# Attention over selected blocks, then a token and channel mixer, on one core: splits and word copies that a planner may put on GpSimd or on VectorE

## The chip, the cores and the metric

The kernel runs on one core of a Trainium2 chip. A core has TensorE (PE, matrix products into PSUM), VectorE (DVE), ScalarE (ACT), GpSimd (POOL) and SyncE (SP, which here only issues DMAs). Each engine takes its instructions from its own queue, in the order in which the program wrote them, and waits for the others through semaphores. The metric is the device time of one execution in microseconds, as the median of several runs.

## The reference

```
q, k, v: [4, 8, 768, 64]                    batch, heads, sequence, head size
kbar  = mean of k over blocks of 64          12 blocks
gate  = q . kbar                             later blocks are left out
sel   = the 3 best blocks of each query, and its own block
attn  = softmax(q k^T / 8 where the key's block is in sel and key <= query)
x     = attn v, heads side by side           [4, 768, 512]
u     = x + (relu(x^T w_tok1) w_tok2)^T
out   = u + relu(u w_ch1) w_ch2
```

## The kernel before

**Pairs.** Two heads of one batch form a pair; there are 16 pairs, number i = 0 to 15, four to a batch. With two heads of 64 channels side by side, a pair's q and k fill 128 partitions once they are transposed. For each pair the kernel loads q, k and v, brings q and k into the layout with channels on partitions, sums k over its blocks, multiplies q by these sums (the gates, tile gps), finds the third largest of the 12 gates of each query (top, tile m), turns "smaller than that" into a bias (bn), transposes the bias, and puts it as 12 extra rows beside q in the tile Q. KA holds k with 12 indicator rows. So the matrix product of KA and Q gives the scores with the mask already in them (sps, L683). ACT takes the exponential (e, L697), PE multiplies by V (aps, L713; a column of ones gives the sum), DVE normalises (rc L721, x L732).

**Mixer.** After the four pairs of a batch come the token mixer (tok1 L756 or L787, umix L768 or L801, uadd L776 or L810) and the channel mixer: a first product (ch1, L837) with relu (L739, L741), and a second one (L888), which is done as seven products of half size per row block, with sums of their operands before (hsum, L869 to L875) and of their results after (keep L745 or L747, vsum L903, vu L910 on POOL, oput L922 and L924, psum L928 and osum L933 on POOL). The mixer of one batch runs between the pairs of the next.

**How k is brought in and split.** Three ways stand side by side:

- Pairs below SPLIT (0 and 1): transposes of f32 data in two halves into PSUM banks (L417), evacuation to f32 tiles kt and qt by ACT or DVE (L443, L445), block sums by DVE into kst, two DVE reductions that write them into the tile ks2 with zeros elsewhere (kcopy, L566), and gates as five f32 matmuls per pair against ks2 (gate_full, L575).
- Pairs from SPLIT to QTURN/KTURN: transposes of six blocks at once into one of the two big PSUM tiles (L409), k evacuated to f32 (L443 or L445), q evacuated as an f16 main part qh (ACT, L458) and an f16 rest qr (DVE, L465). The block sums are split likewise into an f16 main part and an f16 rest in the tile kp (split_k, L549). The gates are ten f16 matmuls (gate_parts, L591), qh and qr against kp.
- Later pairs (q from pair 10, k from 14, the bias from 9): the f16 parts are made before the transposition (L514, L520, L445/L479), which a DMA then does (L399 for u, L525, L640).

kp has a column group for each head of the pair, and a partition of the one head holds zeros in the column group of the other. split_k therefore writes only the 64 x 12 values of each head: four POOL instructions, main part and rest for two heads. The zeros are written once at the start (L1406).

**Word copies.** qh, kh and mt arrive as f16 and must go to the rows of Q and KA. place_q (L546), place_k (L491) and place_m (L646) copy them as f32 words, on POOL.

**Who decides the order.** The kernel first lists all operations, each with an engine, a duration as the planner believes it (occ until the engine is free, rec until the result can be used), its dependencies, a priority and the buffers that it takes. plan() then simulates the engines and picks, step by step, the operation that can start first; among those that can start within NEAR ns of it, the one with the lowest priority value. An operation with an `alt` can go to either of two engines, whichever the plan has done first. `both` marks a DVE operation that the planner does not start before POOL's last instruction has nearly ended. The result is one fixed order per engine; nothing is decided on the chip. PRE (per pair), LAG (per batch) and SHIFT (per kind of operation) move priorities. W0 and WAIT name the copies behind which POOL issues each load of the weights. Dummy matmuls (L963) keep PE busy at the start until 17 us.

Of the kernel before, what the change touches and what calls it, by code (L numbers as in the profile page):

```python
# [45 lines left out]
SHIFT = {'bias': 0.7, 'sc': -0.8999999999999999, 'ex': -2.2, 'uadd': 1.0, 'lt': 4.2, 'ch1': -0.8, 'qn2': 0.0, 'av': 2.8, 'tok1': -11.0, 'gate': -0.5, 'qr': 1.2999999999999998, 'mask': -2.8, 'ksum': -0.3, 'cast': -1.0, 'dg': 2.7, 'half': 1.3, 'top': 0.2, 'put': 0.0, 'kt': -4.0, 'gm': -2.7, 'norm': 4.3999999999999995, 'kcopy': 0.0, 'tr': 0.5, 'v': -0.8, 'relu2': 1.0, 'umix': -0.5, 'relu1': 1.0, 'qh': -6.8, 'qn': -1.5}  # L46
# [17 lines left out]
NEAR = 20.0  # L64
SEED = 0
JITTER = 0.0
SPLIT = 2
# [36 lines left out]
def plan(ops, rings, near=NEAR):  # L104
# [43 lines left out]
    while left:  # L148
# [7 lines left out]
        for e, cand in ready.items():  # L156
# [9 lines left out]
            for op in cand:  # L166
# [51 lines left out]
        if op.both:  # L218
            both_to = t + op.rec
# [31 lines left out]
def kernel(  # L251
# [69 lines left out]
    two = sp.tile([128, 2], F16, tag="two", name="two")  # L321
    spare = sp.tile([128, 8], F16, tag="spare", name="spare")
# [165 lines left out]
    def place_k(i, x):  # L488
        def f():
            lo = 64 * x  # L490
            nc.gpsimd.tensor_copy(out=KA[i % R][x][lo:lo + 64, :].bitcast(FP), in_=T["kh", i][lo:lo + 64, :].bitcast(FP))  # L491
        return f
# [50 lines left out]
    def place_q(i, x):  # L543
        def f():
            lo = 64 * x
            nc.gpsimd.tensor_copy(out=QA[i % R][x][lo:lo + 64, :].bitcast(FP), in_=T["qh", i][lo:lo + 64, :].bitcast(FP))  # L546
        return f

    def split_k(i):  # L549
        def f():  # L550
            kst = T["kst", i]
            t = kp[i % 2]
            for c in range(2):
                for x in range(2):
                    rows = slice(64 * x, 64 * x + 64)
                    hi, lo = t[rows, 1 - x, 0, :], t[rows, 1 - x, 1, :]
                    if c == 0:
                        nc.gpsimd.tensor_copy(out=hi, in_=kst[rows, :])
                    else:
                        nc.gpsimd.tensor_tensor(out=lo, in0=kst[rows, :], in1=hi, op=ALU.subtract)  # L560
# [82 lines left out]
    def place_m(i, x):  # L643
        def f():
# [807 lines left out]
```

## Time and profile before

| | us |
|---|---|
| median of 3 runs | 248.72 (248.71 to 248.92) |
| profiled execution, device time | 249.24 |
| its span, first to last instruction | 247.5 |

The profile is one execution. Its page gives for each engine the busy time and its share of the span; other views of the trace give the same by stages of the span, by line and operation ("L546 POOL COPY Q<-qh 64x384 f32<-64x384 f32 x28" is the copy of line 546, from qh to Q, 64 partitions by 384 words, 28 times, followed by total time, mean in ns, and the idle time of the engine before it with what ended it), and in order of time. A matrix instruction's recorded duration includes its way through the pipeline, so on PE the difference of two starts says what an instruction costs, and the recorded duration says more.

Some shares of the chain of work that ended last:

| by engine | share of the span |
|---|---|
| PE | 67% |
| DMA | 9% |
| POOL | 7% |
| DVE | 5% |
| SP's queue | 4% |
| ACT | 4% |

### The profile page before, as it was taken

How to read it: one execution, taken by the hardware profiler on the slowest of the kernel's cores; microseconds unless marked ns; L12 is line 12 of the kernel's file. 1: busy time of each engine (PE TensorE's matmuls, PEld its weight loads, DVE VectorE, ACT ScalarE, POOL GpSimd, SP SyncE). 2: the span in 40 equal slices, each digit the busy share in tenths (PEclk: the TensorE clock that was granted, in tenths of full speed). 3: DMA queues.
4: the chain of work that ended last, by engine and by line, in shares of the span. 5: the costliest groups of instructions: out<-in, count | busy, mean ns of one | idle time of the engine just before them, and what ended most of it. 6: DMA issues, size and time to landing. Idle time of an engine off the chain costs nothing.

```text
span 247.5 us, 6749 instructions
## 1 busy us (share of the span) xinstructions
PE 237.5 (96%) x2590; PEld 180.2 (73%) x2590; DVE 184.8 (75%) x568; ACT 157.8 (64%) x239; POOL 133.8 (54%) x234
## 2 busy tenths in 40 slices
PE   8998899999999999999999989999999999999994
PEld 6777789877777886687767868658676758756863
DVE  6668569979688997997978999896754659442742
ACT  2778797887996898564566668668759321345210
POOL 8658557369018836577793789994010053800380
PEclk9999999999999999999999999999999999999999
DMA  8999999999993499989999992628200009410033
GB/s 160 211 201 227 185 216 218 216 190 215 230 187 76 103 221 202 192 126 237 231 202 131 213 228 60 157 56 193 47 4 0 3 1 190 153 42 0 3 120 136
DMA packets 106640, 35.78 MB, mean 145 GB/s; under 512 B 100272, under 2 KB 103112, under 8 KB 106608
## 3 DMA queue, kind: packets, MB, share of 16 engines
q1 hardware_dynamic: 101616, 30.84, 62.4%
q0 software_dynamic: 3392, 4.11, 10.1%
q10 hardware_dynamic: 1600, 0.39, 0.8%
q8 instruction: 20, 0.33, 0.6%
q14 instruction: 12, 0.10, 0.1%
HBM read 26.92 MB, written 6.29 MB: 134 GB/s over the span
## 4 chain that ended last, share of the span: by engine, by line
PE 67%; DMA 9%; POOL 7%; DVE 5%; SPq 4%; ACT 4%; issue 2%; POOLq 0%; DVEq 0%; ACTq 0%
PE c L837 24%; PE c L888 13%; PE sps L683 9%; PE aps L713 5%; SPq L360 4%; DMA w<-in_moe_w_tok_dram 3%; DMA ql<-in_q_dram 3%; PE tok L756 3%; POOL vu L910 3%; ACT e L697 3%; DMA v<-in_v_dram 3%; PE tkl L409 2%; PE c L944 2%; PE ups L768 2%; PE tql L409 1%
## 5 line engine op out<-in xcount | busy, mean ns | idle before, releaser
L697 ACT ACTIVATE e<-sps 128x1024 f16<-128x1024 f32 (+2 forms) x96 | 84.7, 918 | 16.7 <-PE sps L683 13.3
L837 PE MATMUL c<-uT,wc 128*128 128x256 f16 (+1 forms) x384 | 68.8, 326 | 0.1
L683 PE MATMUL sps<-Q,KA 76*128 76x128 f16 (+7 forms) x384 | 51.8, 259 | 0.9 <-ACT kt L443 0.3
L910 POOL TENSOR_TENSOR vu<-v,u 128x256 f32<-128x256 f32 x33 | 25.6, 801 | 48.1 <-DVE v L903 46.4
L837 PEld LDWEIGHTS <-wc 128*128 128x128 f16 x384 | 36.4, 98 | 20.4 <-issue 0.5
L683 PEld LDWEIGHTS <-KA 76*128 76x128 f16 (+1 forms) x384 | 30.9, 97 | 14.6 <-issue 1.6
L540 POOL CAST KA<-kt 64x768 f16<-64x768 f32 x26 | 21.8, 837 | 26.5 <-ACT kt L443 22.2
L713 PEld LDWEIGHTS <-e 128*128 128x128 f16 x672 | 24.9, 97 | 2.9 <-issue 0.4
L713 PE MATMUL aps<-V,e 128*128 128x65 f16 x672 | 26.5, 193 | 0.3 <-POOL V L386 0.3
L739 ACT ACTIVATE h2a<-c 128x512 f16<-128x512 f32 (+1 forms) x31 | 16.1, 534 | 13.2 <-PE c L837 13.1
L739 ACT ACTIVATE h2b<-c 128x512 f16<-128x512 f32 (+1 forms) x30 | 15.5, 532 | 11.0 <-PE c L837 10.9
L888 PEld LDWEIGHTS <-s 128*128 128x128 f16 x198 | 18.6, 98 | 2.7 <-DVE s L875 0.3
L386 POOL CAST V<-v 128x768 f16<-128x768 f32 x16 | 14.7, 926 | 7.7 <-DMA v<-in_v_dram 7.0
L732 DVE TENSOR_TENSOR x<-aps,rc 128x384 f16<-128x384 f32 x32 | 17.7, 552 | 0.6
L888 PE MATMUL c<-t,s 128*128 128x256 f16 x132 | 18.0, 272 | 0.0
L703 DVE TENSOR_TENSOR e<-e,m 128x768 f16<-128x768 f16 x24 | 13.8, 575 | 4.8 <-ACT e L697 4.6
L546 POOL COPY Q<-qh 64x384 f32<-64x384 f32 x28 | 16.2, 580 | 2.0 <-ACT qh L458 0.7
L741 DVE TENSOR_SCALAR h2b<-c 128x256 f16<-128x256 f32 (+1 forms) x18 | 8.4, 466 | 9.5 <-PE c L837 9.3
L888 PEld LDWEIGHTS <-h2b 128*128 128x128 f16 x132 | 12.7, 98 | 2.5 <-issue 0.2
L622 DVE MAX8 m<-gps 128x8 f32<-128x12 f32 x160 | 14.0, 161 | 0.4
L613 DVE TENSOR_REDUCE kst<-kt 128x12 f32<-128x768 f32 x13 | 12.3, 944 | 2.6 <-ACT kt L443 2.5
L888 PEld LDWEIGHTS <-h2a 128*128 128x128 f16 x132 | 12.4, 98 | 1.4
(126 smaller groups left out, 428.6 us busy)
## 6 DMA issues: line engine op xcount, KB each, us to landing
v<-in_v_dram SPq DMA_DIRECT2D x16, 384.0 KB, 6.2
out_dram<-ob SPq DMA_DIRECT2D x23, 256.0 KB, 2.2
kl<-in_k_dram SPq DMA_DIRECT2D x30, 192.0 KB, 4.7
ql<-in_q_dram SPq DMA_DIRECT2D x30, 192.0 KB, 4.9
wc<-in_moe_w_ch_dram POOLq DMA_DIRECT2D x8, 384.0 KB, 7.3
w<-in_moe_w_tok_dram POOLq DMA_DIRECT2D x2, 384.0 KB, 6.5
kl<-in_k_dram SPq DMA_DIRECT2D x4, 96.0 KB, 3.2
ql<-in_q_dram ACTq DMA_DIRECT2D x4, 96.0 KB, 3.7
```

Source lines behind the costliest of these rows:

```text
L386: nc.gpsimd.tensor_copy(out=V16[i % (R + 1)][:, :, :, 0:D], in_=T["v32", i])
L540: nc.gpsimd.tensor_copy(out=dst[i % R][x][lo:lo + 64, a:z], in_=T[name, i][lo:lo + 64, a:z])
L546: nc.gpsimd.tensor_copy(out=QA[i % R][x][lo:lo + 64, :].bitcast(FP), in_=T["qh", i][lo:lo + 64, :].bitcast(FP))
L622: nc.vector.max(out=t[:, j, x, :], in_=T["gmx", i, m][:, j, x, :])
L683: nc.tensor.matmul(out=p[:, off + a:off + a + n], lhsT=KA[i % R][x][0:rows, 128 * kk:128 * kk + 128], rhs=QA[i % R][x][0:rows, q0 + a:q0 + ...
L697: nc.scalar.activation(out=e[:, 0:width], in_=T["sps", i, x, g][:, 0:width], func=AF.Exp, scale=scale)
L713: nc.tensor.matmul(out=p[:, jq, :], lhsT=T["e", i, x, g][:, o:o + 128], rhs=V16[i % (R + 1)][:, x, kk, :], start=(kk == 0), stop=(kk == jq))
L732: nc.vector.tensor_tensor(out=T["x16", b][:, :, 64 * hh:64 * hh + 64], in0=T["aps", i, x][:, :, 0:64], in1=T["rc", i, x].broadcast_to([128 ...
L739: e.activation(out=out, in_=src, func=AF.Relu)
L837: nc.tensor.matmul(out=p, lhsT=wc1_16[:, cc, 128 * fc:128 * fc + 128], rhs=T["uT", b][:, a // 128:e // 128, cc, :], start=(cc == 0), stop= ...
L888: nc.tensor.matmul(out=T["c2" + key, b, j], lhsT=x[:, fc, :], rhs=y[:, fc, :], start=first and fc == 0, stop=fc == HF - 1, skip_group_chec ...
L910: nc.gpsimd.tensor_tensor(out=t, in0=T["v", b, j], in1=T["u", b][:, j + 3 * row, 256 * col:256 * col + 256], op=ALU.add)
```

## The change

split_k takes three instructions on all 128 partitions: a product of the block sums with a 0/1 column per head (the new tile half), which puts zeros where the other head's columns are, then the f16 copy, then the rest as a difference. The zeros of kp need no memset any more. split_k, place_q, place_k and place_m become operations of a new kind, flex: planned on POOL, or on DVE where the plan has them done earlier there. For these the rule about DVE and POOL holds where they are planned on DVE. SPLIT goes from 2 to 3, so pair 2 takes the first of the three ways above. NEAR, PRE, LAG and SHIFT have new values.

```diff
-PRE = [3.5, -2.0, -3.0, 0.5, 3.5, 4.0, 5.0, 6.5, -2.5, 0.5, 9.5, 12.5, 3.5, 5.5, -3.0, 2.0]
-LAG = [5.5, 0.0, 3.5, 10.0]
+PRE = [4.0, -1.5, -2.5, 1.0, 3.5, 4.0, 5.0, 6.5, -2.5, 0.5, 9.5, 12.0, 5.5, 7.5, -2.5, 4.0]
+LAG = [5.5, 0.0, 0.5, 7.5]
...
-NEAR = 20.0
+NEAR = 30.0
...
-SPLIT = 2
+SPLIT = 3
...
-                if op.both:
+                if op.both and e == "DVE":
                     t = max(t, pool_to - 140.0)
...
-        if op.both:
+        if op.both and op.eng == "DVE":
             both_to = t + op.rec
...
+    half = sp.tile([128, 2], FP, tag="half", name="half")
...
+    def flex(occ, rec, quick, deps, prio, fn):
+        o = op("POOL", occ, rec, deps, prio, fn)
+        o.alt = ("DVE", quick, quick + 84)
+        o.both = True
+        return o
...
     def split_k(i):
-        def f():
-            kst = T["kst", i]
+        def f(e):
             t = kp[i % 2]
-            for c in range(2):
-                for x in range(2):
-                    rows = slice(64 * x, 64 * x + 64)
-                    hi, lo = t[rows, 1 - x, 0, :], t[rows, 1 - x, 1, :]
-                    if c == 0:
-                        nc.gpsimd.tensor_copy(out=hi, in_=kst[rows, :])
-                    else:
-                        nc.gpsimd.tensor_tensor(out=lo, in0=kst[rows, :], in1=hi, op=ALU.subtract)
+            m = sp.tile([128, 2, NB], FP, tag="ksm", bufs=2, name=f"ksm_{i}")
+            e.tensor_tensor(out=m, in0=T["kst", i].unsqueeze(1).broadcast_to([128, 2, NB]), in1=half.unsqueeze(2).broadcast_to([128, 2, NB]), op=ALU.mult)
+            e.tensor_copy(out=t[:, :, 0, :], in_=m)
+            e.tensor_tensor(out=t[:, :, 1, :], in0=m, in1=t[:, :, 0, :], op=ALU.subtract)
         return f
...
-                O["kcopy", i] = op("POOL", 1040, 998, [O["ksum", i], O.get(("gate", i - 2))], pre + 1, split_k(i))
+                O["kcopy", i] = flex(780, 800, 400, [O["ksum", i], O.get(("gate", i - 2))], pre + 1, split_k(i))
...
-                    O["cast", "qt", i, x] = op("POOL", 457, 503, [O["qh", i]] + zq + last_scores(x), pre + 4.1, place_q(i, x))
+                    O["cast", "qt", i, x] = flex(457, 503, 290, [O["qh", i]] + zq + last_scores(x), pre + 4.1, place_q(i, x))
...
-                    O["put", i, x] = op("POOL", 393, 443, [O["mask", i]] + zq + last_scores(x), pre + 4, place_m(i, x))
+                    O["put", i, x] = flex(393, 443, 270, [O["mask", i]] + zq + last_scores(x), pre + 4, place_m(i, x))
...
-        for r in range(2):
-            nc.vector.memset(kp[r], 0.0)
+        nc.vector.memset(half, 0.0)
+        for n in range(2):
+            nc.vector.memset(half[64 * n:64 * n + 64, 1 - n:2 - n], 1.0)
```

SHIFT changes for bias (0.7 to -2.3), ex (-2.2 to -5.0), uadd (1.0 to -1.2), gm (-2.7 to -5.7), tok1 (-11.0 to -8.0), cast (-1.0 to -2.5), put (0.0 to -1.5) and by half a unit or less for seven more. place_k has the same two edits as place_q.

In the order of instructions that the changed program issues, against the order before: DVE has 439 instead of 404 instructions, POOL 170 instead of 193, ACT 234 instead of 239. The splits of pairs 3, 5, 7, 9, 11, 12 and 15 stand on DVE, those of 4, 6, 8, 10, 13 and 14 on POOL. Of the copies to Q, six of qh (pairs 3, 7, 8, 9, 12, 13, one head each) and six of the bias (both heads of pair 9, one head each of 11, 12, 14 and 15) stand on DVE; the four copies of kh stay on POOL. PE has 10 f16 gate matmuls less with their weight loads, 5 f32 gate matmuls more, and 34 instead of 39 dummies.

More of the change, by code (lines that the diff above doesn't have):

```diff
@@ L1100 @@
                 else:
-                    O["kcopy", i] = op("POOL", 1040, 998, [O["ksum", i], O.get(("gate", i - 2))], pre + 1, split_k(i))
+                    O["kcopy", i] = flex(780, 800, 400, [O["ksum", i], O.get(("gate", i - 2))], pre + 1, split_k(i))
             elif i < SPLIT:
@@ L1118 @@
                 for x in range(2):
-                    O["cast", "qt", i, x] = op("POOL", 457, 503, [O["qh", i]] + zq + last_scores(x), pre + 4.1, place_q(i, x))
+                    O["cast", "qt", i, x] = flex(457, 503, 290, [O["qh", i]] + zq + last_scores(x), pre + 4.1, place_q(i, x))
                     hb.users.append(O["cast", "qt", i, x])
```

16 lines of the change are left out of this document (8 added, 8 removed).

## The prediction

> **What bounds the kernel now.** I read the shares of the engines first, then the same sums by stage of the span, then TensorE's timeline in the stages where it stands idle.
>
> ```profile
> span 247.5 us, 6749 instructions
> PE 237.5 (96%) x2590; PEld 180.2 (73%) x2590; DVE 184.8 (75%) x568; ACT 157.8 (64%) x239; POOL 133.8 (54%) x234
> ```
>
> ```profile
> core 0: us, PE busy (x) PEld busy (x) DVE busy (x) ACT busy (x) POOL busy (x), PEclk, DMA share, GB/s
> 0.00:12.00 12.00, 10.51 (x78) 8.30 (x79) 7.50 (x58) 6.08 (x13) 8.68 (x23) 1.00 1.05 184
> 12.00:36.00 24.00, 21.63 (x313) 17.94 (x312) 16.32 (x66) 19.73 (x26) 15.91 (x28) 1.00 1.14 207
> 36.00:56.00 20.00, 19.08 (x317) 16.70 (x316) 17.21 (x58) 16.72 (x22) 10.72 (x22) 1.00 1.08 208
> 56.00:96.00 40.00, 39.88 (x461) 30.34 (x458) 35.41 (x114) 33.41 (x48) 21.55 (x41) 1.00 0.93 172
> 96.00:136.00 40.00, 39.70 (x385) 28.91 (x384) 34.13 (x92) 24.10 (x42) 26.77 (x45) 1.00 1.01 189
> 136.00:172.00 36.00, 34.46 (x436) 26.71 (x434) 33.39 (x87) 26.24 (x38) 29.66 (x47) 1.00 0.74 149
> 172.00:230.00 58.00, 58.00 (x502) 40.14 (x501) 31.70 (x79) 29.25 (x51) 13.05 (x21) 1.00 0.22 52
> ```
>
> TensorE (PE) is the bound at full clock: from 12 to 230 us it stands idle for 2.37 + 0.92 + 0.12 + 0.30 + 1.54 = 5.25 us, and from 172 to 230 us for none. The change takes most of its work from GpSimd (POOL), which is 54% busy; that can only pay where POOL's lateness reaches PE. So a gain must come out of those 5.25 us, above all from 12-36 and 136-172. The second stage is also where VectorE (DVE) is fullest, 33.39 of 36 us, and DVE receives what POOL gives up.
>
> The waits of PE in the first of the two stages (start, duration, instruction, idle before and releaser):
>
> ```profile
> 14.03 0.71 PE L963 MATMUL warm<-t 128*128 128x256 f16 x5
> 14.71 1.27 PE L575 MATMUL gps<-ks,qt 128*128 128x24 f32 x10
> 15.82 0.85 PE L409 MATMUL tkl<-id,kl 128*128 128x128 f32 x6
> 17.66 0.60 PE L683 MATMUL sps<-Q,KA 128*128 128x384 f16 x4 [0.33 <-ACT kt L443]
> 18.79 0.82 PE L713 MATMUL aps<-V,e 128*128 128x65 f16 x21 [0.26 <-POOL V L386]
> 20.51 0.18 PE L591 MATMUL gps<-kp,qh 128*128 128x48 f16 x1 [0.35 <-POOL kp L560]
> 20.76 0.22 PE L683 MATMUL sps<-Q,KA 76*128 76x128 f16 x1
> 30.24 0.84 PE L787 MATMUL tok<-x,w 128*128 128x128 f16 x12 [0.66 <-DMA w<-in_moe_w_tok_dram]
> ```
>
> The five dummies at 14.03 also stand where PE has nothing to do. In the second stage one wait dominates, and it has a chain that runs through DVE and POOL:
>
> ```profile
> 139.27 2.20 DVE L875 TENSOR_TENSOR s<-h2b,h2a 128x768 f16<-128x768 f16 x1
> 142.09 0.41 DVE L903 TENSOR_TENSOR v<-pa,c 128x256 f32<-128x256 f32 x1
> 143.83 0.41 DVE L924 TENSOR_TENSOR ob<-vu,c 128x256 f32<-128x256 f32 x1
> 147.90 0.57 DVE L875 TENSOR_TENSOR s<-h2b,h2a 128x768 f16<-128x768 f16 x1
> ```
>
> ```profile
> 140.24 0.82 POOL L386 CAST V<-v 128x768 f16<-128x768 f32 x1
> 142.58 2.80 POOL L910 TENSOR_TENSOR vu<-v,u 128x256 f32<-128x256 f32 x3 [1.52 <-DMA ql<-in_q_dram]
> ```
>
> ```profile
> 144.29 0.44 PE L500 MATMUL kps<-two,kn 128*128 128x2 f16 x12 [0.90 <-DVE ob L924]
> ```
>
> The same L875 takes 2.20 us here and 0.57 us at 147.90. The long one ends 0.4 us after POOL's cast ends (141.06 against 141.47). Behind it v (L903) is late, then vu on POOL (put down to a DMA, but v ended 0.08 us before it), then ob (L924), then PE. So a DVE instruction can lose 1.6 us beside POOL, and that reaches PE.
>
> **The change, part by part.** *Splits.* Before, 14 pairs each issue four POOL instructions on 64 partitions; after, 13 pairs each issue three on 128, of which 7 pairs (3, 5, 7, 9, 11, 12, 15) go to DVE and 6 stay.
>
> ```profile
> L546 POOL COPY Q<-qh 64x384 f32<-64x384 f32 x28 | 16.2, 580 | 2.0 <-ACT qh L458 0.7
> L646 POOL COPY Q<-mt 12x320 f32<-12x320 f32 x14 | 7.5, 538 | 7.4 <-DMA mt<-bn 6.7
> L560 POOL TENSOR_TENSOR kp<-kst,kp 64x12 f16<-64x12 f32 x28 | 6.5, 233 | 2.1
> L558 POOL CAST kp<-kst 64x12 f16<-64x12 f32 x28 | 6.4, 230 | 3.4 <-DVE kst L747 1.9 <-DVE kst L613 0.3
> L747 DVE COPY kst<-kps 128x12 f32<-128x12 f32 x2 | 0.3, 158 | 0.0
> L1402 DVE MEMSET Q<- 64x384 uint32 x1 | 0.4, 378 | 0.1
> L747 DVE COPY pd<-c 128x256 f32<-128x256 f32 x2 | 0.8, 410 | 0.0
> L445 DVE TENSOR_SCALAR kn<-kl 128x768 f16<-128x768 f32 x1 | 0.8, 836 | 1.1 <-POOL KA L540 1.1
> ```
>
> On POOL a split costs 2 x 0.23 + 2 x 0.23 = 0.93 us. With 24 values per partition instead of 12 no row shows it; it lies between 0.23 us and the 0.54 us of L646 (320 values), much nearer the first: I take 3 x 0.25 = 0.75. On DVE the nearest is 0.16 us for 128x12, so 3 x 0.16 = 0.48 us, at most 3 x (0.16 + 1.6) beside POOL. POOL is relieved of 12.9 - 6 x 0.75 = 8.4 us, DVE gets 7 x 0.48 = 3.4.
> *Word copies.* Six of the 28 Q copies (L546) and six of the 14 mask copies (L646) go to DVE; the K copies all stay. POOL loses 6 x 0.58 + 6 x 0.54 = 6.7 us. The nearest DVE row of that shape is the memset L1402, 0.38 us; a copy also reads, so 0.38 is a middle, with 0.16 below and 0.38 + 1.6 above. Twelve make 4.6 us.
>
> Here the Trainium skill speaks against the change: its page "SBUF — State Buffer", section "SBUF: two separate sides", says that VectorE and GpSimd share one pair of ports as an exclusive lock, taken by DVE instructions in a two-port mode or with two SBUF inputs, so that the loser waits out the whole instruction. The 2.20 us above agree with it. By it every moved instruction is of the kind that waits, and the outcome would be that of rival 1.
>
> *Pair 2.* With SPLIT at 3 it goes the other way: its transposes fill banks by halves, its gates are five f32 matmuls on ks2 instead of ten f16 ones. For one pair the five cost 15.82 - 14.71 = 1.11 us, the ten 20.76 - 20.51 = 0.25 us: +0.86 us of PE work. In the changed order its K transposes stand ahead of gate 1, where the five dummies ran, so this fills time that was empty; without that cover it costs the 0.86. ACT drops its K evacuation, and DVE does it in two halves.
> *Order.* The new PRE, LAG, SHIFT and NEAR move every queue. Three moves bear on the waits above. (a) No POOL split stands ahead of gate 2 any more, the first P*V stands behind gate 2 and mask 1, and no ACT evacuation of K holds the scores: the 0.33, 0.26 and 0.35 go. (b) The load of w1 is issued right behind POOL's first V cast, where one K cast, the split and a second V cast preceded it:
>
> ```profile
> 17.91 0.82 POOL L386 CAST V<-v 128x768 f16<-128x768 f32 x1 [2.38 <-DMA v<-in_v_dram]
> 22.18 0.88 POOL L992 DMA_DIRECT2D w<-in_moe_w_tok_dram  x1
> ```
>
> That is about 18.7 instead of 22.18, 3.4 us earlier, so it lands near 26.8. The first tok1 also moves up by one transpose, one P*V and one set of scores, some 2.1 us, to 27.5: the 0.66 go with 0.7 us to spare. On POOL's queue V of pair 1 is now behind that issue. (c) On DVE two evacuations and the block sums of pair 2 (together some 1.9 us) now stand ahead of gm of pair 1, so mask 1, its puts and pair 1's scores are late next, by half a microsecond to one.
> Sum for 12-36: gone 0.33 + 0.26 + 0.35 + 0.66 + 0.71 = 2.31, filled by the gates 0.86, leaves 1.45; I give half back for (c) and for ACT, busy 19.73 of 24 us: -0.7 us. Its ends are -1.45 and +0.86.
>
> For 136-172 DVE gets, by the changed order, four word copies (4 x 0.38), three evacuations of products that ACT did (3 x 0.41) and kn of pair 15 (0.84): 3.6 us. Two rest splits (L520) move out of the stage:
>
> ```profile
> 137.32 1.12 DVE L520 SCALAR_TENSOR_TENSOR qn<-ql,qn 128x640 f16<-128x640 f32 x1
> 163.56 1.34 DVE L520 SCALAR_TENSOR_TENSOR qn<-ql,qn 128x640 f16<-128x640 f32 x1
> ```
>
> So DVE comes to 33.39 + 3.6 - 2.5 = 34.5 of 36 us: fuller, not over. POOL has about 2.6 us less there (four copies at 0.56, two splits that are 0.18 shorter), so fewer collisions such as the 2.20. I take the 0.90 as half gone (-0.45) and +0.25 for the fuller DVE: -0.2, between -0.9 and +2.0 (rival 1). The remaining idle, 36-56 and 96-136, I leave. From 172 us on PE does not wait until the last products, whose number stays. The start trades two memsets of kp for four small ones of half and ks; they cost nothing as long as DVE waits for PE behind them:
>
> ```profile
> 5.46 0.56 DVE L437 TENSOR_REDUCE kst<-tkl 128x6 f32<-128x384 f32 x1 [0.63 <-PE tkl L417]
> ```
>
> In all -0.9 us: span 246.6. The profiled execution took 249.24 us, 1.7 around its span; the median of the runs is 248.72, so I forecast **247.8 us**.
>
> **Rivals.** *1. DVE becomes the bound in 136-172 (slower).* Each of the four word copies and kn waits out one POOL instruction of some 0.7 us on average (between L546's 0.58 and L386's 0.82): 34.5 + 5 x 0.7 = 38.0, 2.0 us more than the stage has; what is queued behind them (L776 for tok1, L924 for products) holds PE. With -0.7 from the start that is +1.3: 250.0 us. For it: the 2.20, and L520 at 1.12 and 1.34 us for the same shape. Against: POOL has fewer instructions to collide with. It decides once these waits pass 1.5 us in all. The trace shows such waits in some instructions only, L875 among them, hence 0.28.
>
> By the lock of the Trainium skill's page named above, taken alone, this rival would be the likelier.
> *2. Hidden anyway.* POOL is idle 46%, so its relief reaches no one; the waits of 12-36 reappear at the exponentials of ACT, and the gate's 0.86 just fills them: 248.7 us.
> *3. All waits named go:* -1.45 - 0.9 - 0.5 elsewhere: 245.9 us; the limit is 248.7 - 5.25 - 0.71 + 0.86 = 243.6.
> The change does what it says: the order shows 7 splits and 12 copies on DVE.
>
> **How the numbers follow.** What this kernel can tell from no change is about 0.2%, 0.5 us. Forecast (0.5 to 2 us faster) 0.50, rival 3 0.08, rival 2 0.14, rival 1 0.28. Hence faster 0.58, same 0.14, slower 0.28. The range reaches rival 3 and rival 1: 245.9 to 250.2; the forecast's own is 246.7 to 248.2.
>
> **What would show it.** Right: PE idle in 12-36 near 1.7 instead of 2.37 us, no wait of tok1 for w, POOL near 133.8 - 8.4 - 6.7 = 119 us and DVE near 184.8 + 3.4 + 4.6 + 2.1 (the evacuations and kn) = 195 us in all, moved copies on DVE near 0.4 us. Wrong: mean durations of the moved instructions at twice that, PE waiting for DVE's u, ob or kp after 96 us, POOL no shorter, or the first exponentials of pair 1 later than before.

## The result, and the profile after

The changed kernel takes 251.69 us (median of 6 runs, 250.86 to 252.47), the kernel before 248.72 us: a ratio of 1.0124 with a 95% interval of 1.0095 to 1.0153. It is slower by about 3.0 us. The profiled execution took 250.86 us, the shortest of its runs, so the two traces show 250.86 - 249.24 = 1.6 of the 3.0 us.

The page of the changed kernel, its head and the shares of the engines:

```profile
span 249.1 us, 6722 instructions
PE 238.6 (96%) x2585; PEld 181.1 (73%) x2585; DVE 192.9 (77%) x609; ACT 157.2 (63%) x235; POOL 120.9 (49%) x184
```

```profile
PE 76%; DVE 16%; ACT 4%; issue 2%; POOL 1%; DVEq 0%; ACTq 0%
```

The second line is the chain that ended last, by engine. POOL had 7% of it and DMA 9%, now POOL has 1%; DVE had 5%, now it has 16%. The work went where the change sends it, and the chain now runs through DVE more than through any engine but PE.

Busy time by stage of the changed kernel, the same columns as in the prediction:

```profile
12.00:36.00 24.00, 21.79 (x313) 18.62 (x311) 17.32 (x71) 19.75 (x27) 13.65 (x18) 1.00 1.15 205
36.00:56.00 20.00, 18.64 (x297) 16.08 (x295) 18.89 (x57) 16.42 (x22) 10.29 (x17) 1.00 1.13 212
56.00:96.00 40.00, 39.20 (x467) 30.19 (x466) 36.62 (x112) 33.38 (x47) 19.43 (x30) 1.00 0.96 182
96.00:136.00 40.00, 39.34 (x375) 28.18 (x372) 36.23 (x108) 23.02 (x37) 24.54 (x33) 1.00 0.99 182
136.00:172.00 36.00, 35.21 (x424) 27.11 (x423) 33.84 (x102) 25.46 (x35) 23.10 (x37) 1.00 0.77 138
```

| PE idle in | before | after | forecast |
|---|---|---|---|
| 12-36 us | 2.37 | 2.21 | 1.7 |
| 36-56 | 0.92 | 1.36 | unchanged |
| 56-96 | 0.12 | 0.80 | unchanged |
| 96-136 | 0.30 | 0.66 | unchanged |
| 136-172 | 1.54 | 0.79 | 1.3 |

The two stages that were to gain did gain, 0.16 and 0.75 us. The three that the prediction left alone lost 0.44 + 0.68 + 0.36 = 1.48 us, and in all three DVE is now 91 to 94% busy. (The idle time from 12 to 230 us rose by 0.57 us, the span by 1.6 us; PE's busy time rose as well, by 238.6 - 237.5 = 1.1 us. The f16 gate products of the kernel before start 0.025 us apart and are recorded with 0.18 us each, so busy time can hold part of a wait too. How much of the 1.1 us is waiting and how much is added work is not told apart.)

The largest waits of PE after 36 us that were not there before (releaser in brackets):

```profile
37.12 0.88 PE L416 MATMUL tql<-id,ql 128*128 128x128 f32 x6 [0.78 <-ACT e L699]
...
81.87 0.45 PE L663 MATMUL bps<-id,bn 128*128 128x128 f16 x5 [0.59 <-DVE bn L653]
...
124.29 7.96 PE L839 MATMUL c<-uT,wc 128*128 128x512 f16 x48 [0.65 <-DVE h2a L743]
...
156.31 0.83 PE L715 MATMUL aps<-V,e 128*128 128x65 f16 x21 [0.76 <-DVE x L734]
```

The first is for ACT's exponential and belongs to the new order: the changed order with everything on POOL (e1 below) has it too, and the same 1.36 us of idle time in 36-56.

```profile
36.86 0.88 PE L416 MATMUL tql<-id,ql 128*128 128x128 f32 x6 [0.77 <-ACT e L699]
```

The other three are for DVE, and each stands behind moved operations. With the splits back on POOL (e5) the one at 124 us is gone. With the copies back (e6) those at 82 and 156 us are gone, though PE then waits for a copy on POOL. What DVE did ahead of the wait at 124 us, and what POOL did meanwhile:

```profile
121.89 0.24 DVE L560 TENSOR_TENSOR ksm<-kst,half 128x24 f32<-128x24 f32 x1
122.17 0.85 DVE L561 CAST kp<-ksm 128x24 f16<-128x24 f32 x1
123.05 0.85 DVE L562 TENSOR_TENSOR kp<-ksm,kp 128x24 f16<-128x24 f32 x1
123.83 0.41 DVE L743 TENSOR_SCALAR h2a<-c 128x256 f16<-128x256 f32 x1
124.16 0.20 DVE L560 TENSOR_TENSOR ksm<-kst,half 128x24 f32<-128x24 f32 x1
124.39 0.18 DVE L561 CAST kp<-ksm 128x24 f16<-128x24 f32 x1
124.61 0.18 DVE L562 TENSOR_TENSOR kp<-ksm,kp 128x24 f16<-128x24 f32 x1
```

```profile
120.39 3.48 POOL L547 CAST KA<-kt 64x768 f16<-64x768 f32 x4
123.81 0.51 POOL L553 COPY Q<-qh 64x384 f32<-64x384 f32 x1
```

The split of pair 11 runs beside four POOL casts of 0.87 us each. Its second and third instructions take 0.85 us, the length of a cast. The split of pair 12, a moment later and behind the last of them, takes 0.18 us for the same instructions. The relu h2a stands in DVE's queue behind the first split, and the channel mixer's product on PE stands behind the relu. At 156 us it is the same with a mask copy (L648, 0.87 us) and the diagonal product behind it (L705, 1.46 us) beside POOL's sum, copy and casts. At 82 us a copy to Q (L553) stands ahead of bn and takes 0.36 us, without a collision.

The moved instructions by line, on both engines:

```profile
L553 DVE COPY Q<-qh 64x384 f32<-64x384 f32 x6 | 2.8, 473 | 0.1
L560 DVE TENSOR_TENSOR ksm<-kst,half 128x24 f32<-128x24 f32 x7 | 2.5, 357 | 0.1
L648 DVE COPY Q<-mt 12x320 f32<-12x320 f32 x6 | 2.4, 404 | 0.7 <-DMA mt<-bn 0.6
L562 DVE TENSOR_TENSOR kp<-ksm,kp 128x24 f16<-128x24 f32 x7 | 2.2, 307 | 0.2
L561 DVE CAST kp<-ksm 128x24 f16<-128x24 f32 x7 | 1.9, 274 | 0.2
L560 POOL TENSOR_TENSOR ksm<-kst,half 128x24 f32<-128x24 f32 x6 | 1.6, 274 | 0.1
L562 POOL TENSOR_TENSOR kp<-ksm,kp 128x24 f16<-128x24 f32 x6 | 1.6, 268 | 0.5
L561 POOL CAST kp<-ksm 128x24 f16<-128x24 f32 x6 | 1.4, 239 | 0.4
```

On DVE a split takes 0.357 + 0.274 + 0.307 = 0.94 us on average, though its instructions take 0.18 us each where nothing interferes: 0.4 of the 0.94 us is waiting. A few long ones make it: of the seven casts (L561) the median took 0.178 us, the longest 0.849. On POOL a split takes 0.78 us. So a split that moves to DVE is no shorter there, and the price sits on the fuller engine.

### The profile page after: what moved, and what is told of

Same layout as the page of the kernel before. It is cut to its first block, busy times and chain, and to the rows that moved or that the text cites. A ratio compares the mean times of both kernels' runs of the same rounds, so it can differ in the third digit from the quotient of the medians.

```text
span 249.1 us, 6722 instructions
## 1 busy us (share of the span) xinstructions
PE 238.6 (96%) x2585; PEld 181.1 (73%) x2585; DVE 192.9 (77%) x609; ACT 157.2 (63%) x235; POOL 120.9 (49%) x184
## 4 chain that ended last, share of the span: by engine, by line
PE 76%; DVE 16%; ACT 4%; issue 2%; POOL 1%; DVEq 0%; ACTq 0%
PE c L839 22%; PE c L890 15%; PE sps L685 11%; PE aps L715 6%; PE ups L770 3%; PE tok L758 3%; ACT e L699 2%; PE warm L965 2%; PE c L946 2%; PE tkl L416 2%; DVE qr L472 2%; DVE kst L615 1%; PE gps L577 1%; PE tql L416 1%; DVE x L734 1%
## 5 line engine op out<-in xcount | busy, mean ns | idle before, releaser
L839 PE MATMUL c<-uT,wc 128*128 128x512 f16 (+1 forms) x384 | 68.6, 326 | 0.6 <-DVE h2a L743 0.6
L912 POOL TENSOR_TENSOR vu<-v,u 128x256 f32<-128x256 f32 x33 | 23.8, 747 | 43.3 <-DVE v L905 43.1
L393 POOL CAST V<-v 128x768 f16<-128x768 f32 x16 | 15.6, 978 | 14.6 <-DMA v<-in_v_dram 11.6
L705 DVE TENSOR_TENSOR e<-e,m 128x768 f16<-128x768 f16 x24 | 15.5, 644 | 2.6 <-ACT e L699 2.3
L743 DVE TENSOR_SCALAR h2a<-c 128x256 f16<-128x256 f32 (+1 forms) x19 | 8.2, 432 | 10.0 <-PE c L839 9.9
L553 POOL COPY Q<-qh 64x384 f32<-64x384 f32 x20 | 12.0, 599 | 6.6 <-ACT qh L465 6.0
```

Source lines behind the costliest of these rows:

```text
L393: nc.gpsimd.tensor_copy(out=V16[i % (R + 1)][:, :, :, 0:D], in_=T["v32", i])
L705: nc.vector.tensor_tensor(out=d, in0=d, in1=m0.broadcast_to([128, NJ, 128]), op=ALU.mult)
L743: e.tensor_scalar(out=out, in0=src, scalar1=0.0, scalar2=None, op0=ALU.max)
L839: nc.tensor.matmul(out=p, lhsT=wc1_16[:, cc, 128 * fc:128 * fc + 128], rhs=T["uT", b][:, a // 128:e // 128, cc, :], start=(cc == 0), stop= ...
L912: nc.gpsimd.tensor_tensor(out=t, in0=T["v", b, j], in1=T["u", b][:, j + 3 * row, 256 * col:256 * col + 256], op=ALU.add)
```

## The experiments

Every ratio is against the kernel before, timed on the same chip in the same session.

| kernel | what it is | median us | ratio [95%] |
|---|---|---|---|
| after | the change | 251.69 | 1.0124 [1.0095, 1.0153] |
| e1_order_pool | changed order, all 19 operations back on POOL | 249.81 | 1.0052 [1.0029, 1.0076] |
| e5_splits_back | changed order, 7 splits back on POOL | 249.29 | 1.0022 [0.9997, 1.0047] |
| e6_copies_back | changed order, 12 copies back on POOL | 250.91 | 1.0086 [1.0055, 1.0117] |
| e7_two_back | changed order, 1 split and 1 copy back | 250.63 | 1.0089 [1.0054, 1.0123] |
| e11_three_back | changed order, 3 splits back | 250.21 | 1.0074 [1.0044, 1.0105] |
| e9_gate_twice | the change, pair 2's gates twice | 251.74 | 1.0118 [1.0089, 1.0148] |
| e2_split3 | order of before, new split, all on POOL | 247.75 | 0.9943 [0.992, 0.9966] |
| e18_one_moved | the same, 1 split on DVE | 247.12 | 0.9954 [0.9937, 0.9971] |
| e17_six_moved | the same, 6 splits on DVE | 248.89 | 1.0025 [1.0003, 1.0048] |
| e12_splits_moved | the same, 7 splits on DVE | 249.37 | 1.0041 [1.0016, 1.0065] |
| e3_moved | the same, 7 splits and 12 copies on DVE | 252.82 | 1.0167 [1.0134, 1.0199] |
| e13_told | planned anew, old numbers, new split on POOL | 249.15 | 1.0033 [1.0016, 1.005] |
| e14_told_three | the same with SPLIT 3 | 255.18 | 1.0254 [1.0222, 1.0285] |
| e15_splits_fixed | planned anew, new numbers, splits on POOL alone | 250.15 | 1.0073 [1.0042, 1.0103] |
| e16_fixed_two | the same with SPLIT 2 | 265.40 | 1.0682 [1.0655, 1.071] |
| e4_numbers | new numbers, old split and copies on POOL | 263.76 | 1.0607 [1.0571, 1.0643] |

### The change taken apart: placement, split, order, numbers

**e1_order_pool** keeps the order that the change made on every engine and issues each flexible operation on POOL at its place.

```diff
-                o.fn(engines[o.eng])
+                o.fn(nc.gpsimd if o.both else engines[o.eng])
```

> The changed kernel with its order on every engine, but each split and word copy that stood on DVE is issued on POOL at the same place of the order. Theory 1 (the moved instructions wait for POOL on DVE and hold PE): the waits of 0.81 us at 123.4 and 0.92 us at 155.2 go, and the time falls by 1.5 us or more, to 250.2 us or less. Theory 2 (the new order itself is worse, whatever engine the moved instructions are on): 251.7 us, or slower, as POOL gets 33 instructions back.

Measured 1.0052, which is 0.72% or 1.8 us below the change and still above before. So where the operations run is more than half of the loss, and the changed order keeps a cost of its own. One wait of PE shows what POOL pays for the copies in that order, a wait that the change does not have:

```profile
153.51 0.44 PE L685 MATMUL sps<-Q,KA 76*128 76x128 f16 x5 [1.11 <-POOL Q L648]
```

**e2_split3** is the kernel before with nothing but the new split, on POOL.

```diff
-                    if c == 0:
-                        nc.gpsimd.tensor_copy(out=hi, in_=kst[rows, :])
-                    else:
-                        nc.gpsimd.tensor_tensor(out=lo, in0=kst[rows, :], in1=hi, op=ALU.subtract)
...
+            e.tensor_tensor(out=m, in0=T["kst", i].unsqueeze(1).broadcast_to([128, 2, NB]), in1=half.unsqueeze(2).broadcast_to([128, 2, NB]), op=ALU.mult)
+            e.tensor_copy(out=t[:, :, 0, :], in_=m)
+            e.tensor_tensor(out=t[:, :, 1, :], in0=m, in1=t[:, :, 0, :], op=ALU.subtract)
```

> The kernel before with its order, only each split as three instructions on 128 partitions, all on POOL. Both theories: no change, 248.3 to 249.1 us; POOL's time per split falls from 0.93 to about 0.78 us (0.27 + 0.24 + 0.27), hidden. If the three instructions themselves cost, 249.2 us or more.

Measured 0.9943: faster than before by 1.4 us, and faster than the change by 1.8%. The expectation of no change missed. From its views by line, by stage and in order of time:

```profile
L554 POOL TENSOR_TENSOR ksm<-kst,half 128x24 f32<-128x24 f32 x14 | 3.8, 270 | 3.4 <-DVE kst L743 1.9 <-DVE kst L609 0.9
...
L556 POOL TENSOR_TENSOR kp<-ksm,kp 128x24 f16<-128x24 f32 x14 | 3.5, 249 | 1.1
...
L555 POOL CAST kp<-ksm 128x24 f16<-128x24 f32 x14 | 3.2, 229 | 1.0 <-POOL ksm L554 0.2
```

```profile
136.00:172.00 36.00, 35.99 (x463) 27.93 (x462) 32.32 (x88) 27.21 (x39) 28.52 (x45) 1.00 0.74 147
```

```profile
138.55 0.56 DVE L871 TENSOR_TENSOR s<-h2b,h2a 128x768 f16<-128x768 f16 x1
```

The split takes 0.27 + 0.23 + 0.25 = 0.75 us on POOL instead of 0.93. The sum on DVE that took 2.20 us before (L875 there, L871 here) takes 0.56 us at the same place, and PE's idle time in 136-172 falls from 1.54 to 0.01 us. That the missing collision is the whole gain was not tried by itself.

**e3_moved** takes that kernel and issues on DVE what the change issues there.

```diff
+        moved = {id(O["kcopy", i]) for i in (3, 5, 7, 9, 11, 12, 15)}
+        moved |= {id(O["cast", "qt", i, x]) for i, x in ((3, 0), (7, 1), (8, 1), (9, 1), (12, 0), (13, 0))}
+        moved |= {id(O["put", i, x]) for i, x in ((9, 0), (9, 1), (11, 1), (12, 0), (14, 1), (15, 0))}
...
+            if id(o) in moved:
+                o.fn(nc.vector)
```

> The kernel before with its order and three-instruction splits, and the same set of operations on DVE as in the changed kernel (7 splits, 6 copies of qh, 6 of the bias), each at its old place of the order. Theory 1: 250 us or more, with DVE instructions of 0.8 us and over among the moved ones. Theory 2: 248.3 to 249.2 us.

Measured 1.0167, 2.2% or 5.6 us above e2_split3. In an order that was not made for it the same move costs three times what it costs in the changed order (1.8 us).

**e4_numbers** gives the operations of before the new PRE, LAG, SHIFT, NEAR and SPLIT, and plans anew.

```diff
-NEAR = 20.0
+NEAR = 30.0
...
-SPLIT = 2
+SPLIT = 3
```

> The kernel before with the new PRE, LAG, SHIFT and NEAR and SPLIT at 3, splits and copies all on POOL in the old way, planned anew. Theory 2: 251 us or more. Theory 1: 248.5 to 249.5 us (the gate's 0.86 us of PE included). A plan made for other operations may differ in more than the numbers, so this run alone does not decide.

Measured 1.0607. PE stands idle for 7.15 us in 96-136 us, where it waits for k, u and ob (0.30 us before). The numbers do not suit the old operations; that says nothing of their part in the change.

### Splits or copies

**e5_splits_back, e6_copies_back, e7_two_back and e11_three_back** differ from the changed kernel by one set each of operations that go back to POOL.

```diff
+        back = {id(O["kcopy", i]) for i in (3, 5, 7, 9, 11, 12, 15)}
...
-                o.fn(engines[o.eng])
+                o.fn(nc.gpsimd if id(o) in back else engines[o.eng])
```

In e6 the set is the copies "cast", "qt" and "put", in e7 the split of pair 11 and the put of pair 12, head 0, in e11 the splits of 5, 11 and 12.

> The changed kernel with the seven splits of DVE issued on POOL instead, at the same places; the twelve copies stay on DVE. With all nineteen back the time fell from 251.7 to 249.8 us. Theory (single collisions that reach PE): the split of pair 11 cost PE 0.66 us at 124 us, the other six little, so about 0.7 us less than the changed kernel, 251.0 us (250.6 to 251.4), and the wait of ch1 for h2a at 124 us is gone. Rival (the splits as a whole load DVE): most of the 1.9 us comes back, 250.0 us or less. Rival (only the copies count): 251.5 us or more.

> The changed kernel with the twelve word copies of DVE (six of qh, six of mt) issued on POOL instead; the seven splits stay on DVE. Theory (single collisions): the copy at 152.84 us and the evacuation behind it cost PE 0.76 us at 156 us, the one at 81.15 us up to 0.59, but POOL then makes the copies late by as much as the 1.11 us of Q at 153.5 us that the kernel with all nineteen back shows: 250.9 us (250.2 to 251.4). Rival (the copies' sum of DVE time, 5.2 us, is what counts): 250.0 us or less. Rival (only the splits count): 251.5 us or more.

> The changed kernel with two operations alone issued on POOL instead: the split of pair 11 and the mask copy of pair 12, head 0, the two that stood ahead of PE's largest new waits (0.65 us for h2a at 124 us, 0.76 us for x at 156 us). Theory (single collisions that reach PE set the loss): 0.66 + 0.76 = 1.4 us less than the changed kernel, 250.3 us (249.9 to 250.8). Rival (a collision taken away returns as another one a little later, and POOL's later copies hold the scores): less than 0.5 us gained, 251.2 us or more.

> The changed kernel with three of DVE's seven splits (pairs 5, 11 and 12) issued on POOL instead; those of 3, 7, 9 and 15 and all copies stay on DVE. All seven back gave 249.29 us, 2.5 us less than the changed kernel. Theory (a split costs where a relu of the mixer is queued behind it on DVE and the next product of PE waits for that relu: h behind split 5 at 51.2 us, h2a behind splits 11 and 12 at 123.8 us): these three carry most of it, 249.7 us (249.2 to 250.2). Rival (each split costs its share of DVE time): 3/7 of 2.5, 250.7 us. Rival (as with two back, a wait taken away returns elsewhere): 251.0 us or more.

e5 measured 1.0022: the seven splits carry 1.0% or 2.5 us. The first rival of its expectation held: the splits as a whole, not the one of pair 11. e6 measured 1.0086, 0.9 us below the change, with intervals that overlap. With the splits on POOL no cost of the copies can be told: e5 has them on DVE, e1 has not, and e5 is 0.3% lower, with intervals that overlap. The wait of 1.11 us for POOL's mask copy may be why: it is in e1 and in e6, and gone where that copy runs on DVE.

e7 removed two operations that stood ahead of waits of 0.65 and 0.76 us, 1.4 us in all, and got 0.9 us. e11 got 1.2 us where the theory asked for 2 and a mere share for 1.1. The intervals of both overlap that of the change, so the two gains are rough. In e11's trace, as in that of e7, PE has a new wait instead:

```profile
102.27 1.19 PE L770 MATMUL ups<-h,w 128*128 128x512 f16 x4 [0.63 <-DVE u L778]
```

### The same split in the order of before

**e12_splits_moved** is e3_moved without the two lines for the copies; **e17_six_moved** leaves out pair 12 from its set, **e18_one_moved** has pair 12 alone. The edit of e17 against e12:

```diff
-        moved = {id(O["kcopy", i]) for i in (3, 5, 7, 9, 11, 12, 15)}
+        moved = {id(O["kcopy", i]) for i in (3, 5, 7, 9, 11, 15)}
```

> The order of before with three-instruction splits, of which the same seven as in the change are issued on DVE; all copies stay on POOL. With all splits on POOL this order took 247.75 us, with the seven splits and the twelve copies on DVE 252.82. Theory (a split costs what is queued behind it): in the profile with both on DVE one wait of PE of 0.96 us stood behind splits, waits of 1.20, 0.51 and 0.53 us behind copies, so the splits alone make 0.9 to 2.0 us, 249.2 us (248.6 to 249.8). Rival (the splits are the harm in any order, as 2.5 of the 3 us in the changed order): 250.3 us or more. Rival (they hide here): 248.1 us or less.

> The order of before with three-instruction splits, six on DVE (pairs 3, 5, 7, 9, 11, 15), the split of pair 12 back on POOL. With all seven on DVE the time was 1.0041 of before, and PE waited 1.77 us at 128.8 us for the relu h2a that stood behind split 12. Theory (that one split carries most): 1.2 to 1.8 us less, a ratio of 0.997 to 0.9995, with no such wait. Rival (the loss is DVE's load, seven splits share it): 0.3 to 0.5 us less, 1.002 or more.

> The order of before with three-instruction splits, that of pair 12 alone on DVE, all else on POOL. With none on DVE the ratio was 0.9943, with seven 1.0041. Theory (this one split, 0.54 us of DVE work, costs 1.2 us or more because PE waits for the relu behind it): a ratio of 0.999 or more, with a wait of PE for h2a of more than 1 us near 129 us. Rival (a single split on DVE hides): 0.996 or less.

e12 is 1.0% above e2_split3, 2.4 us, nearly what the splits cost in the changed order. Its own timeline shows the same place as in the change, with the relu behind a split beside POOL's casts:

```profile
126.28 0.78 DVE L554 TENSOR_TENSOR ksm<-kst,half 128x24 f32<-128x24 f32 x1
127.10 0.42 DVE L555 CAST kp<-ksm 128x24 f16<-128x24 f32 x1
127.56 0.85 DVE L556 TENSOR_TENSOR kp<-ksm,kp 128x24 f16<-128x24 f32 x1
128.34 0.41 DVE L737 TENSOR_SCALAR h2a<-c 128x256 f16<-128x256 f32 x1
```

```profile
128.80 3.62 PE L833 MATMUL c<-uT,wc 128*128 128x512 f16 x20 [1.77 <-DVE h2a L737]
```

e17 takes that split away. The stages of e17, the last two before the long final stretch:

```profile
96.00:136.00 40.00, 40.00 (x387) 29.12 (x385) 35.39 (x96) 23.60 (x41) 26.98 (x40) 1.00 0.99 189
136.00:172.00 36.00, 34.93 (x437) 27.10 (x435) 32.58 (x90) 26.49 (x39) 29.48 (x44) 1.00 0.78 148
```

PE is no longer idle in 96-136 us, so the 1.77 us are gone where they stood. But 1.07 us of idle time are now in 136-172, where e12 had 0.13, and the time falls by only 0.16% or 0.4 us. e18 puts only this split on DVE: 0.9954 against 0.9943, a cost that cannot be told from none. Both theories that give one split a price of 1.2 us or more fell. The rival, that the seven share the loss, is nearer.

What remains in line with the runs in this order is the load of DVE, in which the waits beside POOL count. DVE's busy time is 183.6 us in e2, 184.7 in e18, 188.9 in e17, 191.0 in e12 and 194.7 in e3, and the ratios rise in the same order. Seven splits need 7 x 3 x 0.18 = 3.8 us when undisturbed, but e12's DVE is 191.0 - 183.6 = 7.4 us busier than e2's. Among the placements in the changed order it is the same but for one pair: e1 has 184.4 us and 1.0052, e5 187.9 us and 1.0022. From one order to the other it does not carry over: e1 has nearly the load of e18 and is 1% slower. That DVE's load sets the loss, rather than something that goes with it, was not tried separately.

### Pair 2 through the f32 gates

**e9_gate_twice** issues pair 2's five f32 gate products twice.

```diff
-            for j in range(a, z):
+            for j in [*range(a, z)] * (1 + (i == 2)):
```

> The changed kernel with the five f32 gate matmuls of pair 2 issued twice in a row (the same result written twice), to price what pair 2's way through the f32 gates costs at the start: five take 1.19 us of PE there (17.79 to 18.98 us). Theory (at the start PE's waits behind them, 0.46 and 0.66 us, are for DVE and ACT that themselves follow these gates, so nothing hides them): at least 0.9 us more than the changed kernel, 252.6 us or more. Rival (they fill time in which PE would wait, as the prediction half assumed): 0 to 0.5 us more, 251.7 to 252.2 us.

Measured 1.0118 against 1.0124: no cost of the second five can be told, to within the 0.3% of each interval. That the first five are hidden as well follows from it only by argument. From its view of PE in order of time:

```profile
18.12 2.36 PE L577 MATMUL gps<-ks,qt 128*128 128x24 f32 x20
...
125.43 7.96 PE L839 MATMUL c<-uT,wc 128*128 128x512 f16 x48 [0.63 <-DVE h2a L743]
```

At 125 us PE is still 125.43 - 124.29 = 1.1 us late against the change. At the tok1 product that starts at 159.04 us in the change 0.3 us are left (159.32), and the wait of 0.76 us at 156 us is gone. So a delay of 1.1 us at the start was paid out of a later wait.

### Planned anew

**e13_told** tells the planner of before that the new split, on POOL alone, takes 780 and 800 ns; **e14_told_three** adds SPLIT 3. **e15_splits_fixed** is the changed kernel with the splits planned for POOL alone, **e16_fixed_two** the same with SPLIT 2.

```diff
-                O["kcopy", i] = op("POOL", 1040, 998, [O["ksum", i], O.get(("gate", i - 2))], pre + 1, split_k(i))
+                O["kcopy", i] = op("POOL", 780, 800, [O["ksum", i], O.get(("gate", i - 2))], pre + 1, split_k(i))
```

> The order of before planned anew, with the three-instruction split on POOL alone and its shorter price (780 and 800 ns instead of 1040 and 998) told to the planner; old numbers, SPLIT 2, every copy on POOL. With the same split in the old order it took 0.9943 of before. Theory (the split's shortness is the gain, the order is secondary): within 1.2 us of that, 246.3 to 248.6 us. Rival (the old order was fitted to the old numbers, any new plan loses): 249.5 us or more.

> As e13_told, but pair 2 goes through the f32 gates too (SPLIT 3), still under the old numbers. Theory (pair 2's f32 way costs the start 0.9 us or more, beyond what dummies gave): 0.9 to 2 us above e13_told. Rival (it fills time that was empty, as doubling its gates cost nothing): within 0.5 us of e13_told. A plan that collapses in some later stage, as the new numbers with the old operations did in 96-136 us, tells neither.

> The changed kernel, planned anew with the splits allowed on POOL alone (780 and 800 ns); word copies may still go to DVE, 13 do. Theory (the changed order keeps a cost because it was planned for splits on DVE): a plan that knows where they run gets 1 to 2 us below the same placement in the changed order (249.3 us), 247.3 to 248.3 us. Rival (the numbers or SPLIT 3 carry the cost): 249 us or more.

> As e15_splits_fixed, but SPLIT at 2, so pair 2 takes the f16 way again. Theory (SPLIT 3 carries the order's cost): 1 to 2 us below e15_splits_fixed. Rival (it carries none): within 0.5 us of it or above it.

e13 issues the operations of e2 in another order, a few evacuations on the other engine, and is 0.9% or 2.2 us slower, between the theory and the rival of its expectation. e15 has the splits where e5 has them, and its planner knew it: 0.5% slower than e5, with intervals that just overlap; the gain that its theory asked for did not come. e14 and e16 lose 5.5 and 15 us more, e14 with one wait of 2.85 us for x (L728) at 161 us; plans that are so much worse in one stage say nothing of SPLIT. So the plans differ among themselves by as much as the changed order costs (e1 less e2, 1.1% or 2.7 us), and these runs cannot put that cost down to SPLIT or to a single number. That stays open.

### What an instruction on DVE pays beside POOL

**e8_alone_beside** and **e10_in_order** measure it directly: twelve of each kind of instruction alone, then beside POOL casts of 128x768.

```
for n in range(10 * N): gpsimd.tensor_copy(out=cw, in_=wide)
for n in range(N):      vector.tensor_copy(out=b, in_=dst[:, 0:24])
```

> Not the model: a kernel that leaves all of the computation out (it writes zeros) and measures single instructions. Seven kinds of DVE instruction, twelve of each, first with POOL idle and then beside an unbroken row of POOL casts of 128x768 f32 to f16 (about 0.82 us each): the f32 copy 64x384 in SBUF, the cast 128x24 in SBUF, the difference 128x24 of two SBUF tiles, a reduction 128x768 to 128x12, the f16 sum 128x768 of SBUF tiles, a sum with one operand in PSUM, a copy out of PSUM. Theory (single-source copies and casts within SBUF wait for POOL as sums of two SBUF operands do): alone 0.34, 0.18, 0.18, 0.94, 0.57, 0.41, 0.41 us; beside POOL the copy, the cast, the difference and the f16 sum take up to a POOL instruction more (0.5 to 1.2, 0.5 to 1.0, 0.5 to 1.0, 0.7 to 1.4 us), the reduction and the two with PSUM stay as they are, and POOL's casts get longer beside the four as well. Rival (only instructions with two SBUF operands wait): the copy and the cast keep 0.34 and 0.18 us. Rival (no wait of this kind, only slower memory): all seven get longer by a similar share.

> Not the model: all of the computation is left out (zeros are written). The seven kinds of DVE instruction again, now twelve of one kind in a row, each kind depending on the one before, first with POOL idle, then beside an unbroken row of POOL casts of 0.83 us. With the kinds mixed, the cast of 128x24 took 0.16 us behind a reduction and 0.80 us behind an f16 sum. Theory (DVE and POOL take the SBUF access in turns, one instruction each): in a row every small cast, difference, word copy and f16 sum beside POOL waits, a cast then takes 0.8 us on average, a word copy 0.9 or more, a sum 1.1 or more; the reduction and the two with PSUM keep 0.94, 0.41, 0.41. Rival (DVE keeps the access as long as its instructions follow each other closely): the first of a row waits, the others take what they take alone, so the mean is within 0.1 us of alone and POOL's casts are held instead, up to the length of a row. Rival (a single-source cast or copy never waits by itself, it only ends late behind a sum): casts and copies in a row stay at 0.16 and 0.34.

In e8 the instructions of different kinds were mixed in the order that ran, and the word copies ran before POOL began, so it decides nothing about them. The small cast took 0.16 us behind a reduction and 0.80 us behind an f16 sum. e10 fixes the order. Its groups by line, the first of each pair alone, the second beside POOL:

```profile
L71 DVE TENSOR_TENSOR sums<-hf 128x768 f16<-128x768 f16 x12 | 12.2, 1017 | 0.4
L55 DVE TENSOR_REDUCE red<-sums 128x12 f32<-128x768 f16 x12 | 11.4, 953 | 0.4
L73 DVE TENSOR_REDUCE red<-sums 128x12 f32<-128x768 f16 x12 | 11.4, 953 | 0.4
...
L65 DVE COPY dst<-acc 64x384 f32<-64x384 f32 x12 | 9.8, 817 | 0.4
L53 DVE TENSOR_TENSOR sums<-hf 128x768 f16<-128x768 f16 x12 | 6.7, 558 | 0.4
L69 DVE TENSOR_TENSOR hf<-dst,b 128x24 f16<-128x24 f32 x12 | 5.9, 492 | 0.4
L67 DVE CAST b<-dst 128x24 f16<-128x24 f32 x12 | 5.2, 431 | 0.4
...
L75 DVE TENSOR_TENSOR acc<-bank,red 128x256 f32<-128x256 f32 x12 | 5.1, 424 | 0.4
...
L47 DVE COPY dst<-src 64x384 f32<-64x384 f32 x12 | 4.2, 351 | 0.4
L51 DVE TENSOR_TENSOR hf<-dst,b 128x24 f16<-128x24 f32 x12 | 2.2, 182 | 0.4
L49 DVE CAST b<-dst 128x24 f16<-128x24 f32 x12 | 2.1, 178 | 0.4
```

| kind on DVE | alone us | beside POOL casts |
|---|---|---|
| word copy 64x384 (L47, L65) | 0.35 | 0.82 |
| cast 128x24 (L49, L67) | 0.18 | 0.43 |
| difference 128x24 (L51, L69) | 0.18 | 0.49 |
| f16 sum 128x768 (L53, L71) | 0.56 | 1.02 |
| reduction 128x768 (L55, L73) | 0.95 | 0.95 |
| sum with one operand in PSUM (L57, L75) | 0.42 | 0.42 |
| copy out of PSUM (L59, L77) | 0.42 | 0.42 |

Copies, casts and sums within SBUF wait, none longer than 0.67 us, which is less than one POOL cast of 0.83; the reduction and what reads PSUM do not. The theory had the kind right, and the size too high for the cast (0.8 us expected, 0.43 measured) and the word copy (0.9 and 0.82). That shows the kind of the wait: the word copies, the cast and the difference that the change moves are of the waiting sort, while the relus and evacuations out of PSUM queued behind them are not. (The split's first instruction, a product of two SBUF operands, was not measured by itself.) Waits inside the kernel can be longer: the product took up to 1.21 us in e12, the sum 2.20 us before. The rival by which only two-operand instructions wait fell with the copy, the rival of a memory that is slower for all fell with the reduction, and the rival by which a row of DVE instructions waits once fell with the means. The Trainium skill, page "SBUF — State Buffer", section "SBUF: two separate sides", describes an exclusive lock on a shared pair of ports; e10 agrees with it in what waits (0.82 against 0.35 us) and in what does not (0.42 and 0.42).

## Why the prediction was wrong

Forecast were 247.8 us (245.9 to 250.2) and a gain; it came out at 251.69 us and a loss.

**The step that failed first** is "The remaining idle, 36-56 and 96-136, I leave". The moved instructions and the new order reach all stages, but only 12-36 and 136-172 had a term for them. Those left out, 56-96 included, lost 1.48 us of PE's time, more than the 0.91 us that the other two gained. In 56-96 and 96-136 the loss comes from the moved operations: PE is idle there for 0.80 and 0.66 us, and for 0.20 and 0.20 with all of them back on POOL in the same order (e1). DVE was 85 to 89% busy in these two stages before, a little less than the 93% of 136-172, the only stage for which the prediction reckoned DVE's load. In 36-56 the loss comes from the order, as the wait for ACT above shows.

**The second** is the price of a split on DVE, "3 x 0.16 = 0.48 us, at most 3 x (0.16 + 1.6) beside POOL". Undisturbed it is 3 x 0.18 = 0.54, so the row was well chosen; measured are 0.94 us, and in the changed order seven of them cost 2.5 us of the total (e5). The collision was seen, with its 2.20 us, and was put into the bound and a rival of 0.28; the price of a split in the sum had none of it. The prediction had named twice its durations as a sign of being wrong, and 0.94 is twice 0.48. The copies were nearer: 0.38 forecast, 0.47 and 0.40 measured, and no cost that can be told while the splits stay on POOL.

**The third** is the part on the order, which was credited with a net gain, -0.7 us in 12-36. With everything on POOL the changed order and SPLIT at 3 together cost 2.7 us (e1 less e2). This is the largest term of the loss, and which of the new numbers carries it stays open.

**Rival 1** had the mechanism: moved instructions that wait out POOL. It had the wrong place, 136-172, where PE gained. It counted four copies and kn, where all twelve copies and 21 split instructions are of that kind, and its 250.0 us fall short by 1.7. The argument against it, "POOL has fewer instructions to collide with", held in part only. The sums L875 (L877 after) fell from 8.7 to 6.7 us in all and the rest splits L520 (L527 after) from 6.9 to 5.0, nearly as far as in e1 (6.7 and 5.5), which points to the order rather than to the moves. But POOL's long casts stayed, and the moved splits ran beside them. Nor does the 2.20 us agree in size with the rule set beside it, by which an instruction waits out one of the other engine: the 1.6 us lost are about twice POOL's 0.82.

**12-36:** -0.7 forecast, -0.16 by idle time. The named waits went as forecast, and tok1 waits no more for w. In their place PE waits for x and for ACT's exponentials, which took back more than the half that the prediction allowed. Rival 2 had named the exponentials; (c) had named mask 1 and what follows from it:

```profile
21.70 0.84 PE L715 MATMUL aps<-V,e 128*128 128x65 f16 x21 [0.46 <-DVE x L734]
...
24.52 0.59 PE L685 MATMUL sps<-Q,KA 128*128 128x512 f16 x3 [0.66 <-ACT e L699]
```

The +0.86 for pair 2's gates was set against empty time; e9 speaks for that and does not show it.

**136-172:** -0.2 forecast, -0.75 by idle time; the wait of 0.90 us went altogether, and one of 0.76 us came at another place.

**Right** were POOL's load, 119 us forecast and 120.9 measured, and the split on POOL at 0.75 and 0.78 us. DVE's load, 195 and 192.9, came near by luck: the moved instructions took 11.8 us there instead of 3.4 + 4.6 = 8.0, and the rest of DVE's work, which was to grow by 2.1 us, fell by 3.7.

**Missing from the sum** were two terms of opposite sign: what the shorter split gains where it is (1.4 us, e2) and the 2.7 us of the order. The third part is the placement, 1.8 us (the change less e1), in which the splits lose and the mask copies perhaps gain. -1.4 + 2.7 + 1.8 = 3.1 us is the whole by construction, since each part is a difference of two of these kernels; it is no check of the parts.

## What to carry to other kernels

Price an instruction that moves to VectorE with the wait beside GpSimd's casts in the sum, for every stage that receives one, when it reads and writes SBUF only; beside an unbroken row of casts a short one took 2.4 to 2.7 times its length (e10), and a split in the change 1.7 times. Do not add up waits of TensorE as if each were a gain: taking away one of 1.77 us brought 0.4 us, and 1.1 us more of work at the start showed no cost. When a change bundles an edit with a new order, run the edit in the old order first: here the three-instruction split on GpSimd alone has the lowest ratio, 0.9943 of before, with one split on DVE (0.9954) not told apart from it.

## What the runs showed of the hardware

- A cast of 24 values per partition on DVE takes 0.18 us alone and 0.43 us on average beside POOL casts of 0.83 us (e10). A reduction of 768 values within SBUF keeps its 0.95 us.
- POOL loses little in this contest (e10): its casts took 0.83 us alone and 0.85 us on average beside DVE, at most 1.25.
- Which of the two goes first in a mixed sequence is not settled. In e8 an f16 sum right behind a small cast never waited (0.54 us beside POOL and alone), while in e10 a sum behind a sum took 1.02 us.
